# Retention, soft mixture of experts and a bilinear layer on one core: the first pair's k ahead of its tables, and the logits' exponential ahead of PV

## The chip, the cores and the metric

The kernel runs on one core of a Trainium2 chip. The core has five engines with an instruction row each: TensorE (PE; PEld is its weight load), VectorE (DVE), ScalarE (ACT), GpSimd (POOL) and SyncE (SP), which here issues the transfers; 16 DMA engines carry these. An engine takes its instructions strictly in the order in which they were written. The metric is the device time of one execution in microseconds (us).

## The reference

What is computed, cut to what matters (8 batches, 8 heads, 576 positions of 64 features, so 4608 tokens of 512):

```python
scores = np.matmul(q, k.transpose(0, 1, 3, 2)) / np.sqrt(64)
ret = scores * Dmat            # gamma_h ** (i - j) for i >= j, else 0
x = np.matmul(ret, v)          # then (4608, 512): tokens x (heads * 64)

logits = x @ phi               # 32 slots
d = np.exp(logits - logits.max(0)); d /= d.sum(0) + 1e-09
slot_input = d.T @ x           # 8 experts x 4 slots
for e in range(8):
    slot_out[e] = np.maximum(slot_input[e] @ w1[e], 0) @ w2[e]
c = np.exp(logits - logits.max(1, keepdims=True)); c /= c.sum(1, keepdims=True) + 1e-09
x = c @ slot_out

out = (((x @ m1) * (x @ m2)) @ w3) @ w_out
```

The weights m1, m2, w3 and w_out come as 64-bit floats and are converted on the chip (`conv_list`).

## The kernel before, in words

**Stages.** First the retention stage runs over 36 units of 128 tokens. Then the eight experts run over the 32 slots, with a product of w3 and w_out (`emit_Ws`) between them; then a small stage on the slots' pair products (`L955`, `L979`), and last nine output blocks of 512 tokens (`L1018` to `L1023`).

**Units.** A unit holds two chunks of 64 positions of one batch, all heads. Two units that hold the same chunks of two batches are a pair, and share one load each of q, k and v (512 KB each). Four pairs and one tail unit (the ninth chunk of both batches) make a group of 9 units; there are four groups. For a unit u TensorE does: `emit_kt` (four transposes of the scaled k, `L202`, copied to `kt` by ACT, `L203`), `emit_qk` (`L234`), masked by VectorE into `pm` (`emit_p`, `L244`), `emit_pv` (`L262`, into banks 5 and 3), `emit_state` (the running k-v product, `L275`, copied by ACT, `L282` or `L285`) and `emit_inter` (that state by q, `L295`, into banks 5 and 3 for the next unit). VectorE multiplies banks 5 and 3 by the factor table of the block into `xts` (`emit_xt`, `L308`); so `L295` must wait for `L308`. `emit_xtr` transposes `xts` and ACT copies it to `xg`.

**Scaling of k.** The raw rows of a pair, `kr` (two buffers), are multiplied by powers of gamma from the small table `ktab_sb` into `k` (`scale_k`: VectorE for the first pair, else GpSimd, `L189`, with ACT for two of the blocks, `L194`). A buffer of `kr` is free for load_k two pairs later when this is done. `xtab_sb` holds the factor tables of four blocks, made by GpSimd (`L659`) from the first and from `xstab`, a copy of the state table `stab_sb` with the two halves of the partitions swapped in every second column.

**Logits.** Every fourth unit, at the end of unit u with r = 1, `emit_logits` puts the logits of 512 tokens in one of three rotating banks (`misc_bank`), VectorE takes their running maximum and its negative `nm` (`L336` to `L343`). In the next unit (r = 2; u = 6, 10, ... 34) `emit_exp` on ACT makes the exponential `dd`, the correction `al` and the copy `lga` (`L357`), which is the last reader of the bank. The transposes of `emit_kt` of the unit after that need this bank.

**What sets the order.** `tc.manual_schedule()`: each engine's row is the order of the code. In every unit the loop emits, besides the above, pieces of the weight conversion (ACT `L469`, `L471`; VectorE `L470`, `L472`, `L464`; GpSimd `L490`, `L500`), and SP's requests for the pair three ahead and for the next weights. The expert weights go into the buffers that the retention stage leaves.

Of the kernel before, what the change touches and what calls it, by code (L numbers as in the profile page):

```python
# [15 lines left out]
ACTF = mybir.ActivationFunctionType  # L16
# [5 lines left out]
NU = NTOK // 128  # L22
# [9 lines left out]
def retention_softmoe_bilinear(  # L32
# [74 lines left out]
    ktab_sb = tabs_sb[:, 128:160].rearrange("p (c h k) -> p c h k", c=4, h=2)  # L107
# [238 lines left out]
    def emit_exp(T, keep=True):  # L346
        ps, nm, mn = st["lg"]
        lg = ps[:, 0:128]
        dd = tmp.tile([128, 128], F32, tag="dd", name="dd")
        zt = tmp.tile([128, 1], F32, tag="zt", name="zt", bufs=2)  # L350
        nc.scalar.activation(out=dd, in_=lg, func=ACTF.Exp, bias=nm, scale=1.0, accum_out=zt)
        al = None
        if T > 0:
            al = tmp.tile([128, 1], F32, tag="al", name="al", bufs=2)
            nc.scalar.activation(out=al, in_=st["m"], func=ACTF.Exp, bias=nm, scale=1.0)
        if keep:
            nc.scalar.copy(out=lga[:, T], in_=lg)  # L357
        st["m"] = mn
        st[T] = (dd, al, zt)
# [250 lines left out]
    with tc.manual_schedule():  # L610
        for i in range(2):
            for h in range(2):
                r = 64 * (1 - h)
                nc.sync.dma_start(out=ktab_sb[i:128:2, :, h], in_=tabs[r:r + 64, 256:292].rearrange("p (c k) -> p c k", k=4)[:, i:8:2])
        load_k(0)
        nc.sync.dma_start(out=cst[:, 0:160], in_=consts)
        load_q(0)
        nc.sync.dma_start(out=stab_sb, in_=tabs[:, 292:328].rearrange("p (c k) -> p c k", c=9))
        load_v(0)
        for r in range(2):  # L620
            for a, b in ((lo, hi), (hi, lo)) if r else ((slice(0, 128),) * 2,):
# [5 lines left out]
        for a, b in ((lo, hi), (hi, lo)):  # L627
            nc.sync.dma_start(out=ptail[a], in_=tabs[b, 0:256].rearrange("p (k i) -> p k i", k=4))
        for r in range(2):
            for a, b in ((lo, hi), (hi, lo)) if r else ((slice(0, 128),) * 2,):  # L630
                nc.sync.dma_start(out=phi_sb[a, r::2], in_=phi[b, r::2])
        nc.vector.memset(acc, 0.0)
        late = acc[:, 128:256]
# [29 lines left out]
        emit_kt(2)  # L663
# [13 lines left out]
        for u in range(NU):  # L677
            T, r = divmod(u - 4, 4)
            if first_of_pair(u + 4):
                scale_k(u + 4)  # L680
                load_k(pairs_in_order.index(units[u + 4][0]) + RBUF)
# [5 lines left out]
            if u + 3 < NU:  # L687
                emit_kt(u + 3)
            emit_pv(u)
            emit_xt(u)  # L690
            if u + 1 < NU:
                emit_state(u + 1)
            if u + 2 < NU:
# [23 lines left out]
            if u >= 6 and r == 2:  # L717
                emit_exp(T)
# [383 lines left out]
```

## Time and profile before

| | |
|---|---|
| timed runs | 429.08, 428.30, 425.40 us; median 428.3 |
| profiled execution | 425.7 us, its span 424.0 us |
| TensorE busy | 393.7 us (93%) |
| VectorE, ACT, GpSimd busy | 252.0, 198.2, 167.6 us |
| mean DMA rate | 255 GB/s |

The span runs from the first to the last instruction of the profiled execution. Busy time counts an engine's instructions; a matmul's end is modelled, since matmuls are pipelined. A releaser ("<-") is the work whose end let a waiting engine go on.

### The profile page before, as it was taken

The page shows a single profiled execution, that of the slowest core. Times are in us where ns is not written, and L with a number is a line of the kernel's source. Part 1 is how long each engine was busy: PE and PEld are TensorE (multiplying, and loading weights), DVE is VectorE, ACT ScalarE, POOL GpSimd, SP SyncE. Part 2 cuts the span into 40 slices and gives each one's busy share as a digit, 9 for nine tenths or more (in the row PEclk, how much of TensorE's full clock was granted, in tenths as well). Part 3 has the DMA queues.
Part 4 walks back from the last instruction along what each step waited for, and adds up shares of the span by engine and source line. Part 5 has one row for each costly group of instructions (what it writes and reads, how often), then busy time and mean ns, then how long its engine had stood idle before and what let it go on. Part 6 is the DMA issues. An engine that isn't in the chain of part 4 may idle for free.

```text
span 424.0 us, 11525 instructions
## 1 busy us (share of the span) xinstructions
PE 393.7 (93%) x4727; PEld 297.3 (70%) x4727; DVE 252.0 (59%) x492; ACT 198.2 (47%) x415; POOL 167.6 (40%) x149
## 2 busy tenths in 40 slices
PE   5589898999899898989999988899999999999996
PEld 2478786887777787866565544376888888888884
DVE  3335889788788886843777655048954443444310
ACT  2033677667656666532544432124454444545431
POOL 0151476564425444322344433102744434443410
PEclk9589999999999999999999999999999999999999
DMA  5889899779867967789899999967064898879633
GB/s 150 179 271 349 271 324 346 249 248 362 291 224 258 339 253 245 271 275 403 308 400 411 408 409 408 358 158 147 1 147 102 222 232 221 185 209 238 166 85 90
DMA packets 53076, 108.24 MB, mean 255 GB/s; under 512 B 12608, under 2 KB 15168, under 8 KB 53024
## 3 DMA queue, kind: packets, MB, share of 16 engines
q1 hardware_dynamic: 53024, 107.51, 79.1%
q8 instruction: 37, 0.61, 0.6%
q14 instruction: 15, 0.12, 0.1%
HBM read 96.87 MB, written 10.62 MB: 254 GB/s over the span
## 4 chain that ended last, share of the span: by engine, by line
PE 38%; DMA 10%; DVE 1%; ACT 1%; SPq 1%; issue 0%; ACTq 0%
PE bank L1018 8%; PE bank L1019 8%; PE bank L1020 8%; PE bank L955 5%; DMA k<-in_ew 5%; PE bank L531 3%; DMA kt<-in_ew 2%; DMA v<-in_ew 2%; PE bank L1021 2%; PE bank L577 2%; PE bank L558 1%; DMA lga<-expt 1%; PE bank L979 1%; DVE w L540 0%; SPq L592 0%
## 5 line engine op out<-in xcount | busy, mean ns | idle before, releaser
L602 POOL TENSOR_TENSOR cc<-mw_sb,cc 128x512 fp32r<-128x512 f32 x36 | 46.3, 1297 | 56.4 <-ACT cc L601 56.4
L490 POOL TENSOR_TENSOR vals<-vals,msb 128x512 int32<-128x512 int32 x24 | 30.8, 1283 | 59.5 <-DVE vals L464 34.5
L244 DVE TENSOR_TENSOR pm<-bank,msb 128x512 f32<-128x512 f32 x64 | 41.2, 684 | 16.9 <-PE bank L234 16.9
L600 DVE TENSOR_TENSOR mw_sb<-lga,raw 128x512 f32<-128x512 f32 x32 | 29.9, 956 | 34.9 <-POOL cc L602 28.4
L531 PE MATMUL bank<-wop,w3p 128*128 128x512 f32 x192 | 50.5, 406 | 0.0
L1023 ACT ACTIVATE mw_sb<-bank,rz 128x512 f32<-128x512 f32 x36 | 24.8, 689 | 51.4 <-PE bank L1021 28.9
L531 PEld LDWEIGHTS bank<-wop,w3p 128*128 128x128 f32 x192 | 34.2, 188 | 15.1 <-issue 8.7
L321 ACT COPY xg<-bank 128x512 f32<-128x512 f32 x34 | 19.9, 587 | 52.8 <-PE bank L320 52.7
L1018 PE MATMUL bank<-w3p,cc 128*128 128x512 f32 x108 | 42.4, 392 | 0.0
L1019 PE MATMUL bank<-w3p,cc 128*128 128x512 f32 x108 | 42.2, 391 | 0.0
L1020 PE MATMUL bank<-w3p,cc 128*128 128x512 f32 x108 | 42.2, 390 | 0.0
L234 PE MATMUL bank<-q,kt 64*64 64x128 f32 x1024 | 38.3, 285 | 1.1 <-DVE pm L244 0.8
L490 POOL TENSOR_TENSOR mw_sb<-mw_sb,msb 128x512 int32<-128x512 int32 x16 | 20.4, 1274 | 40.2 <-DVE mw_sb L464 31.2
L262 PE MATMUL bank<-pm,v 128*64 128x128 f32 x512 | 36.0, 283 | 0.1
L189 POOL TENSOR_TENSOR k<-kr,msb 128x512 f32<-128x512 f32 (+1 forms) x30 | 25.4, 866 | 23.5 <-DMA kr<-in_v 23.5
L202 PE MATMUL bank<-cst,k 128*128 128x128 f32 x128 | 21.1, 290 | 13.9 <-ACT lga L357 6.8
L500 POOL TENSOR_TENSOR w3p<-vals,w3p 128x512 fp32r<-128x512 f32 x16 | 20.5, 1283 | 33.6 <-ACT w3p L495 33.6
L234 PEld LDWEIGHTS bank<-q,kt 64*64 64x64 f32 x1024 | 29.7, 138 | 4.6 <-DVE pm L244 1.5
L262 PEld LDWEIGHTS bank<-pm,v 128*64 128x64 f32 x512 | 28.1, 139 | 5.9 <-issue 5.6
L471 ACT ACTIVATE msb<-raw 128x512 int32<-128x512 uint32 x40 | 27.8, 695 | 0.0
L202 PEld LDWEIGHTS bank<-cst,k 128*128 128x128 f32 x128 | 14.8, 146 | 17.9 <-ACT lga L357 6.3
L601 ACT CAST cc<-mw_sb 128x512 fp32r<-128x512 f32 x36 | 21.6, 618 | 11.4 <-DVE mw_sb L600 8.7
(190 smaller groups left out, 783.7 us busy)
## 6 DMA issues: line engine op xcount, KB each, us to landing
q<-in_q SPq DMA_DIRECT2D x20, 512.0 KB, 6.2
raw<-expt SPq DMA_DIRECT2D x36, 256.0 KB, 4.3
kr<-in_v SPq DMA_DIRECT2D x16, 512.0 KB, 5.5
v<-in_v SPq DMA_DIRECT2D x16, 512.0 KB, 6.8
raw<-in_m SPq DMA_DIRECT2D x16, 512.0 KB, 6.8
raw<-in_w SPq DMA_DIRECT2D x16, 512.0 KB, 6.2
out_x<-mw_sb SPq DMA_DIRECT2D x64, 128.0 KB, 2.8
k<-in_ew SPq DMA_DIRECT2D x14, 512.0 KB, 10.0
```

Source lines behind the costliest of these rows:

```text
L202: nc.tensor.transpose(ps[:, 128 * p:128 * p + 128], k_tile(u)[:, x, p].rearrange("p h j -> p (h j)"), ident)
L234: nc.tensor.matmul(out=ps[b, p], lhsT=ktb[u % 2][a, p, b], rhs=Q[a, :, x, p], start=True, stop=True)
L244: nc.vector.tensor_tensor(out=p_main(u)[:, h], in0=qk_view(h).rearrange("p (k t) -> p k t", k=4), in1=mask_sb.unsqueeze(1).to_broadcast([1 ...
L262: nc.tensor.matmul(out=xt_view(p)[side(p, h)], lhsT=v_tile(u)[:, 1 - h, x, p], rhs=p_main(u)[:, h, p], start=(block_of(u) == 0 and p < 2), ...
L471: lambda: nc.scalar.activation(out=p.bitcast(I32), in_=lo, func=ACTF.Copy, scale=2.0 ** -29),
L490: nc.gpsimd.tensor_tensor(out=ti, in0=ti, in1=parts[j % 2].bitcast(I32), op=ALU.add)
L531: nc.tensor.matmul(out=ps, lhsT=x, rhs=y, start=(k8 == 0 and part == 0), stop=(k8 == 7 and part == 2))
L600: eng.tensor_tensor(out=e, in0=x, in1=y[:, m], op=ALU.mult)
L602: nc.gpsimd.tensor_tensor(out=cl[m], in0=e, in1=ch[m], op=ALU.subtract)
L1018: nc.tensor.matmul(out=ob, lhsT=ch[m][:, sl], rhs=gh[m], start=(m == 0), stop=False)
L1019: nc.tensor.matmul(out=ob, lhsT=ch[m][:, sl], rhs=gl[m], start=False, stop=False)
L1020: nc.tensor.matmul(out=ob, lhsT=cl[m][:, sl], rhs=gh[m], start=False, stop=False)
```

## The change

It moves instructions and changes small transfers; the amount of arithmetic stays, but for one memset and two tables' multiplications that change engines.

At the start: SP's first request is the k of pair 0. The tables for k's scaling come in runs of 32 numbers (all blocks and both kinds of heads at once, of which every second is used) and, like the identity, by ACT's queue; the state table comes whole, in three transfers instead of four, and the swapped copy's even columns are copied by GpSimd. The second pair's k is requested fourth. The tail tables and phi are requested behind the third pair's loads. VectorE scales all four blocks of the first pair, in two halves, with the transposes of a half right behind it. The first unit's PV stands ahead of the second pair's transposes. A dummy exponential makes ACT load its table early.

In the loop: `emit_exp` stands ahead of `emit_pv` of its unit, and its copy `lga` ahead of `al`.

```diff
@@ the tables of k's scaling
-    ktab_sb = tabs_sb[:, 128:160].rearrange("p (c h k) -> p c h k", c=4, h=2)
+    ktab_rows = tabs_sb[:, 240:304].rearrange("p (h n) -> p h n", h=2)
+    ktab_sb = tabs_sb[:, 240:304].rearrange("p (h c i k) -> p c h i k", h=2, c=4, i=2)[:, :, :, 0]
@@ emit_exp
+        if keep:
+            nc.scalar.copy(out=lga[:, T], in_=lg)
         if T > 0:
             al = tmp.tile([128, 1], F32, tag="al", name="al", bufs=2)
             nc.scalar.activation(out=al, in_=st["m"], func=ACTF.Exp, bias=nm, scale=1.0)
-        if keep:
-            nc.scalar.copy(out=lga[:, T], in_=lg)
@@ ahead of the loop
+        load_k(0)
         for i in range(2):
             for h in range(2):
                 r = 64 * (1 - h)
-                nc.sync.dma_start(out=ktab_sb[i:128:2, :, h], in_=tabs[r:r + 64, 256:292].rearrange("p (c k) -> p c k", k=4)[:, i:8:2])
-        load_k(0)
-        nc.sync.dma_start(out=cst[:, 0:160], in_=consts)
+                nc.scalar.dma_start(out=ktab_rows[i:128:2, h], in_=tabs[r:r + 64, 256 + 4 * i:288 + 4 * i])
+        nc.scalar.dma_start(out=cst[:, 0:160], in_=consts)
         load_q(0)
-        nc.sync.dma_start(out=stab_sb, in_=tabs[:, 292:328].rearrange("p (c k) -> p c k", c=9))
         load_v(0)
+        load_k(1)
...
-                nc.sync.dma_start(out=xstab[a, :, r::2], in_=tabs[b, 292:328].rearrange("p (c k) -> p c k", c=9)[:, :, r::2])
-        load_k(1)
+                nc.sync.dma_start(out=(xstab if r else stab_sb)[a], in_=tabs[b, 292:328].rearrange("p (c k) -> p c k", c=9))
         load_q(1)
         load_v(1)
...
+        nc.scalar.activation(out=zacc, in_=acc[:, 0:1], func=ACTF.Exp)
...
-        scale_k(0, True)
+        first_k = rb[0].rearrange("p (h x k j) -> p h x k j", h=2, x=2, k=4)
+
+        def scale_first(x):
+            for h in range(2):
+                nc.vector.tensor_tensor(
+                    out=k_tile(0)[:, x, :, h], in0=first_k[:, 1 - h, x], in1=ktab_sb[:, 0, h].unsqueeze(2).to_broadcast([128, 4, 64]), op=ALU.mult,
+                )
+
+        scale_first(0)
+        emit_kt(0)
+        scale_first(1)
         load_k(2)
-        load_q(2)
-        load_v(2)
+        emit_kt(1)
...
-        nc.vector.memset(acc, 0.0)
-        emit_kt(0)
-        emit_kt(1, nc.vector.tensor_copy)
+        load_q(2)
+        load_v(2)
...
         emit_qk(0)
         emit_p(0)
-        nc.vector.tensor_tensor(
-            out=xtab_sb[0][:, :, 64:128], in0=xtab_sb[0][:, :, 0:64], in1=xstab[:, 1].unsqueeze(2).to_broadcast([128, 4, 64]), op=ALU.mult,
-        )
-        scale_k(2)
-        load_k(3)
-        for c in range(1, 4):
-            nc.gpsimd.tensor_tensor(out=xtab_sb[c], in0=xtab_sb[0], in1=xstab[:, 2 * c].unsqueeze(2).to_broadcast([128, 4, 128]), op=ALU.mult)
         emit_qk(1)
         emit_p(1)
         emit_state(0)
-        emit_kt(2)
+        nc.gpsimd.tensor_copy(xstab[:, :, 0::2], stab_sb[:, :, 0::2])
+        scale_k(2)
+        load_k(3)
+        for c in range(4):
+            o, n = (64, 64) if c == 0 else (0, 128)
+            nc.gpsimd.tensor_tensor(
+                out=xtab_sb[c][:, :, o:o + n], in0=xtab_sb[0][:, :, 0:n], in1=xstab[:, max(2 * c, 1)].unsqueeze(2).to_broadcast([128, 4, n]), op=ALU.mult,
+            )
@@ the loop over units (scale_k and load_k of unit u + 4 are next_k now, which unit 0 calls behind emit_kt(3))
-            if u + 3 < NU:
+            if 0 < u < NU - 3:
                 emit_kt(u + 3)
+            if u >= 6 and r == 2:
+                emit_exp(T)
             emit_pv(u)
+            if u == 0:
+                emit_kt(2)
             emit_xt(u)
             if u + 1 < NU:
                 emit_state(u + 1)
+            if u == 0:
+                emit_kt(3)
+                next_k()
...
-            if u >= 6 and r == 2:
-                emit_exp(T)
```

The places at which engines wait or are waited for, as rows of instructions (line numbers of the changed kernel are its own). SP's row at the very start of the program, before (kr_107 and kr_108 are the two buffers for raw k, q_101, q_102 and v_104, v_105 those of the first two pairs; msb holds the small tables, slotm the first factor table, cst the identity):

```order
L614 DMA msb<-in_tabs 64x4x4 x4
L162 DMA kr_107<-in_v 128x2x512
L616 DMA cst<-in_consts 128x160
L172 DMA q_101<-in_q 128x2x512
L618 DMA msb<-in_tabs 128x36
L178 DMA v_104<-in_v 128x2x512
L622 DMA slotm<-in_tabs 128x2x64
L623 DMA msb<-in_tabs 128x18x1
L622 DMA slotm<-in_tabs 64x2x64
L623 DMA msb<-in_tabs 64x18x1
L622 DMA slotm<-in_tabs 64x2x64
L623 DMA msb<-in_tabs 64x18x1
L162 DMA kr_108<-in_v 128x2x512
```

and in the changed kernel:

```order
L163 DMA kr_107<-in_v 128x2x512
L173 DMA q_101<-in_q 128x2x512
L179 DMA v_104<-in_v 128x2x512
L163 DMA kr_108<-in_v 128x2x512
L624 DMA slotm<-in_tabs 128x2x64
L625 DMA msb<-in_tabs 128x36
L624 DMA slotm<-in_tabs 64x2x64
L625 DMA msb<-in_tabs 64x36
L624 DMA slotm<-in_tabs 64x2x64
L625 DMA msb<-in_tabs 64x36
L173 DMA q_102<-in_q 128x2x512
L179 DMA v_105<-in_v 128x2x512
```

The second pair's k (kr_108) stood behind all tables and stands fourth now; the tables for k and the identity have left this row.

TensorE's row behind the `emit_qk` of units 0 and 1, before (bank_72 and bank_70 are the banks 5 and 3 of PV, bank_71 the state, bank_69 and bank_73 the rotating ones; v_104 is pair 0, k_110 the second pair's scaled k, pm_97 unit 0's masked product):

```order
L275 MATMUL bank_71<-v_104,k_109 64x64 x8
L202 MATMUL bank_69<-cst,k_110 128x128 x4
L202 MATMUL bank_73<-cst,k_110 128x128 x4
L262 MATMUL bank_72<-pm_97,v_104 64x128 x2
L262 MATMUL bank_70<-pm_97,v_104 64x128 x2
L262 MATMUL bank_72<-pm_97,v_104 64x128 x2
L262 MATMUL bank_70<-pm_97,v_104 64x128 x2
L275 MATMUL bank_71<-v_104,k_109 64x64 x8
```

and in the changed kernel:

```order
L276 MATMUL bank_71<-v_104,k_109 64x64 x8
L263 MATMUL bank_72<-pm_97,v_104 64x128 x2
L263 MATMUL bank_70<-pm_97,v_104 64x128 x2
L263 MATMUL bank_72<-pm_97,v_104 64x128 x2
L263 MATMUL bank_70<-pm_97,v_104 64x128 x2
L203 MATMUL bank_69<-cst,k_110 128x128 x4
L276 MATMUL bank_71<-v_104,k_109 64x64 x8
L203 MATMUL bank_73<-cst,k_110 128x128 x4
```

The second pair's eight transposes stood ahead of unit 0's PV, and stand behind it and behind `emit_state(1)` now.

ACT's row around the exponential of unit 10, before (kt from bank_74 is the copy of unit 13's transposes, xg_96 that of `emit_xtr`):

```order
L203 COPY kt<-bank_74 128x512
L321 COPY xg_96<-bank_69 128x512
L351 ACTIVATE dd,zt<-bank_73,nm 128x128
L355 ACTIVATE al<-mt,nm 128x1
L357 COPY lga<-bank_73 128x128
L471 ACTIVATE msb<-raw 128x512
L194 ACTIVATE k_110<-kr_108,msb 128x2x64 x2
L495 CAST wop<-vals 128x512
```

and in the changed kernel:

```order
L204 COPY kt<-bank_74 128x512
L352 ACTIVATE dd,zt<-bank_73,nm 128x128
L355 COPY lga<-bank_73 128x128
L358 ACTIVATE al<-mt,nm 128x1
L322 COPY xg_96<-bank_69 128x512
L472 ACTIVATE msb<-raw 128x512
L195 ACTIVATE k_110<-kr_108,msb 128x2x64 x2
L496 CAST wop<-vals 128x512
```

The exponential and the copy lga stood behind the xg copy, and stand right behind the kt copy now, lga ahead of al.

## Rows read from the trace of the kernel before

**Rows 1.** The page: busy us of each engine (share of the span) and instructions.

```profile
PE 393.7 (93%) x4727; PEld 297.3 (70%) x4727; DVE 252.0 (59%) x492; ACT 198.2 (47%) x415; POOL 167.6 (40%) x149
```

**Rows 2.** Timeline, 0 to 28 us: start, length, engine, line, work, [idle before <-releaser].

```profile
0.80 2.77 SPq L614 DMA_DIRECT2D msb<-in_tabs  x4
...
7.86 4.10 SPq L622 DMA_DIRECT2D slotm<-in_tabs  x1
...
8.95 0.44 PE L202 MATMUL bank<-cst,k 128*128 128x128 f32 x2 [2.01 <-DVE k L189]
...
10.24 0.58 ACT L203 COPY kt<-bank 128x512 f32<-128x512 f32 x1 [0.42 <-PE bank L202]
...
10.88 1.99 PE L234 MATMUL bank<-q,kt 64*64 64x128 f32 x32 [0.24 <-ACT kt L203]
...
14.07 0.72 SPq L162 DMA_DIRECT2D kr<-in_v  x1
...
16.14 1.12 PE L275 MATMUL bank<-v,k 128*64 128x64 f32 x16
...
19.43 1.61 POOL L189 TENSOR_TENSOR k<-kr,msb 128x512 f32<-128x512 f32 x2 [17.18 <-DMA kr<-in_v]
...
21.10 1.97 PE L202 MATMUL bank<-cst,k 128*128 128x128 f32 x8 [3.84 <-POOL k L189]
...
27.35 0.66 PE L202 MATMUL bank<-cst,k 128*128 128x128 f32 x4 [1.07 <-POOL k L189]
```

**Rows 3.** Windows: length, then busy us of each engine, PEclk, DMA share, GB/s.

```profile
10.00:11.00 1.00, 0.76 (x9) 0.52 (x13) 0.59 (x2) 0.58 (x1) 0.00 (x0) 0.91 1.10 323
12.00:16.00 4.00, 3.22 (x50) 2.33 (x44) 1.29 (x2) 0.00 (x0) 0.00 (x0) 0.50 0.50 22
17.30:21.10 3.80, 0.00 (x0) 0.00 (x1) 1.44 (x3) 0.69 (x2) 1.67 (x3) 0.50 1.02 364
21.10:24.24 3.14, 3.14 (x20) 2.81 (x22) 0.00 (x0) 0.59 (x1) 2.94 (x3) 0.50 0.83 251
23.00:186.00 163.00, 153.13 (x3301) 126.25 (x3304) 127.28 (x263) 99.33 (x226) 77.01 (x72) 1.00 0.83 285
```

**Rows 4.** TensorE's waits from 23 to 186 us: total, times, longest.

```profile
PE bank L202 <- ACT lga L357: 6.8, 5, 1.5
PE bank L295 <- DVE xts L308: 1.7, 2, 1.3
```

**Rows 5.** The chain that ended last: its first transfer of the expert stage.

```profile
227.51 10.14 DMA v<-in_ew
```

**Rows 6.** Windows again, in the expert stage.

```profile
205.00:210.00 5.00, 4.67 (x41) 2.19 (x44) 4.83 (x11) 2.87 (x7) 2.58 (x2) 1.00 0.67 241
```

**Rows 7.** Groups by form, 0 to 23 us: xcount, busy us, mean ns, idle before.

```profile
L659 POOL TENSOR_TENSOR slotm<-slotm,msb 128x512 f32<-128x512 f32 x1 | 1.0, 1042 | 0.0
...
L189 DVE TENSOR_TENSOR k<-kr,msb 128x256 f32<-128x256 f32 x1 | 0.4, 418 | 0.0
```

**Rows 8.** DMA issues up to 9 us: count, size, median us to landing.

```profile
kr<-in_v SPq DMA_DIRECT2D x1, 512.0 KB, 4.1
...
cst<-in_consts SPq DMA_DIRECT2D x1, 80.0 KB, 3.9
msb<-in_tabs SPq DMA_DIRECT2D x4, 4.0 KB, 2.2
...
msb<-in_tabs SPq DMA_DIRECT2D x1, 9.0 KB, 5.9
```

**Rows 9.** Timeline of units 10 and 11, and of unit 19 (last row).

```profile
67.48 0.15 DVE L343 TENSOR_SCALAR nm<-mn 128x1 f32<-128x1 f32 x1
...
71.72 0.26 ACT L357 COPY lga<-bank 128x128 f32<-128x128 f32 x1
...
72.18 1.66 DVE L464 SCALAR_TENSOR_TENSOR vals<-raw,vals 128x512 uint32<-128x512 uint32 x1
...
109.55 0.69 DVE L464 SCALAR_TENSOR_TENSOR mw_sb<-raw,mw_sb 128x512 uint32<-128x512 uint32 x1
```

More of the change, by code (lines that the diff above doesn't have):

```diff
@@ L610, in retention_softmoe_bilinear @@
     with tc.manual_schedule():
+        swap = lambda r: ((lo, hi), (hi, lo)) if r else ((slice(0, 128),) * 2,)
+        load_k(0)
         for i in range(2):
@@ L613, in retention_softmoe_bilinear @@
                 r = 64 * (1 - h)
-                nc.sync.dma_start(out=ktab_sb[i:128:2, :, h], in_=tabs[r:r + 64, 256:292].rearrange("p (c k) -> p c k", k=4)[:, i:8:2])
-        load_k(0)
-        nc.sync.dma_start(out=cst[:, 0:160], in_=consts)
+                nc.scalar.dma_start(out=ktab_rows[i:128:2, h], in_=tabs[r:r + 64, 256 + 4 * i:288 + 4 * i])
+        nc.scalar.dma_start(out=cst[:, 0:160], in_=consts)
         load_q(0)
-        nc.sync.dma_start(out=stab_sb, in_=tabs[:, 292:328].rearrange("p (c k) -> p c k", c=9))
         load_v(0)
+        load_k(1)
         for r in range(2):
-            for a, b in ((lo, hi), (hi, lo)) if r else ((slice(0, 128),) * 2,):
+            for a, b in swap(r):
                 nc.sync.dma_start(out=xtab_sb[0][a, r::2, 0:64], in_=tabs[b, 328:584].rearrange("p (k i) -> p k i", k=4)[:, r::2])
-                nc.sync.dma_start(out=xstab[a, :, r::2], in_=tabs[b, 292:328].rearrange("p (c k) -> p c k", c=9)[:, :, r::2])
-        load_k(1)
+                nc.sync.dma_start(out=(xstab if r else stab_sb)[a], in_=tabs[b, 292:328].rearrange("p (c k) -> p c k", c=9))
         load_q(1)
         load_v(1)
[L627 to L631, printed above, removed]
         nc.vector.memset(acc, 0.0)
+        nc.scalar.activation(out=zacc, in_=acc[:, 0:1], func=ACTF.Exp)
         late = acc[:, 128:256]
@@ L647, in retention_softmoe_bilinear @@
         nc.vector.scalar_tensor_tensor(out=mask_sb, in0=mask_sb, scalar=even, in1=late, op0=ALU.mult, op1=ALU.add)
-        nc.vector.memset(acc, 0.0)
-        emit_kt(0)
-        emit_kt(1, nc.vector.tensor_copy)
+        load_q(2)
+        load_v(2)
+        for a, b in swap(1):
+            nc.sync.dma_start(out=ptail[a], in_=tabs[b, 0:256].rearrange("p (k i) -> p k i", k=4))
+        for r in range(2):
+            for a, b in swap(r):
+                nc.sync.dma_start(out=phi_sb[a, r::2], in_=phi[b, r::2])
         emit_qk(0)
         emit_p(0)
-        nc.vector.tensor_tensor(
-            out=xtab_sb[0][:, :, 64:128], in0=xtab_sb[0][:, :, 0:64], in1=xstab[:, 1].unsqueeze(2).to_broadcast([128, 4, 64]), op=ALU.mult,
-        )
-        scale_k(2)
-        load_k(3)
-        for c in range(1, 4):
-            nc.gpsimd.tensor_tensor(out=xtab_sb[c], in0=xtab_sb[0], in1=xstab[:, 2 * c].unsqueeze(2).to_broadcast([128, 4, 128]), op=ALU.mult)
         emit_qk(1)
@@ L678, in retention_softmoe_bilinear, with next_k @@
             T, r = divmod(u - 4, 4)
-            if first_of_pair(u + 4):
-                scale_k(u + 4)
-                load_k(pairs_in_order.index(units[u + 4][0]) + RBUF)
+            def next_k():
+                if first_of_pair(u + 4):
+                    scale_k(u + 4)
+                    load_k(pairs_in_order.index(units[u + 4][0]) + RBUF)
+            if u > 0:
+                next_k()
             run(subs)
@@ L692, in retention_softmoe_bilinear @@
                 emit_state(u + 1)
+            if u == 0:
+                emit_kt(3)
+                next_k()
             if u + 2 < NU:
```

## The prediction

> **What bounds the kernel now.** I read the page's busy times first [rows 1]: TensorE is busy for 393.7 of 424.0 us, so a change gains only where TensorE stands still or runs at its lower clock. Next, the timeline of the first 28 us [rows 2]: TensorE ends its first piece of work (the transposes of units 0 and 1, both `emit_qk`, `emit_state(0)`) at 16.14 + 1.12 = 17.26 and then stands still for 3.84 us, until GpSimd has scaled the second pair's k, for which GpSimd in turn waited for the transfer. That k was requested only at 14.07: SyncE had four row tables to issue ahead of the first k (2.77 us), and later one table whose issue took 4.10 us. Unit 1 waits another 1.07 us for the third pair's k. The windows [rows 3] show what the queue was doing: from 12 to 16 us the DMA engines are busy for half the time and move 22 GB/s, against 364 GB/s from 17.3 to 21.1. That is where the state tables for `xstab` come in, in runs of 4 bytes. The same windows show the granted clock: 0.91 between 10 and 11 us, and still 0.50 (the lower level, 1.2 GHz) from 21.1 to 24.24, at the end of which it rises, TensorE having worked without a gap since 21.10.
>
> Behind that, the waits of TensorE from 23 to 186 us [rows 4] are nearly all that is left to gain in the retention stage: 6.8 us in five waits of a transpose `L202` for ACT's copy `L357`, and 1.7 us for `L308`. With the 1.07 us above this agrees with the row over that stage [rows 3]: TensorE busy for 153.1 of 163 us.
>
> Last, the chain of waits: from 227.5 us it goes through transfers of expert weights, some 10 us each [rows 5], so the expert stage is bound by DMA. Does it absorb what the first stage gains? Its transfers start when TensorE frees a buffer; from 205 to 210 us the DMA engines are busy for 0.67 of the time [rows 6], so until then it is not DMA that sets the pace. The saturated part begins when the work ahead lets it, and moves earlier as a whole. I take a shift of the first stage as a shift of the end, one for one.
>
> **The change part by part.** *The wait for the second pair's k: 3.84 us.* load_k(1) is now SP's fourth issue; at the 0.7 us that each of the four tables took to issue (2.77), it is issued by about 2.8. Behind k, q and v, 2.1 MB in all at 364 GB/s from about 2.9, it lands at 9 to 10. Also, PV(0) no longer stands behind its transposes in TensorE's row, and needs only P(0) and the first pair's v. The 3.84 us go entirely.
>
> *The start of the chain: 1.2 us.* The first transposes began at 8.95, and qk(0) at 10.88, right behind the copy of kt(0) (0.58). Now the scaling is four VectorE multiplications of 256 elements at 0.42 [rows 7], of which the first two release kt(0); ACT's two are gone. k(0) is issued at 0.8 and lands 4.1 us later [rows 8], at 4.9; ktab goes out on ACT's queue, four issues in 2.8 us, landing 2.2 us behind the last [rows 8], at about 5.6. Scaling of x = 0 is done by 6.6. Then the identity, which the transposes need, comes last: fifth in ACT's queue, issued at about 3.6. With its old 3.9 us [rows 8] it lands at 7.5. But it now shares the engines with 2.1 MB instead of with k(0) alone; were it served only after all of that, it would land at 10.0. I take 8.2, near the first, because at its old place it also had 512 KB ahead of it. Four transposes at 0.22 (two took 0.44) end at 9.1, and qk(0) begins at 9.7, 1.2 us earlier. Bounds: 1.9 earlier to 0.7 later. The copy of kt(1) moves from VectorE to ACT, behind that of kt(0): 0.58 us, wanted only by qk(1), so nothing.
>
> The Trainium skill, page "DMA: Bandwidth & Descriptors", section "Issuing engines are not separate DMA queues", says that transfers started by different engines end up on the same 16 DMA engines and interleave, so that a second issuing engine saves only the time of issuing. No trace here shows a second queue. By that rule what ACT's queue brings is SP's 2.77 us, and the identity's transfer is drawn out by what it interleaves with; the first rival works that out from rows.
>
> *The clock: 1.5 us.* If it falls at 10.9 again, qk(0), begun at 9.7, has 1.2 us at the full clock ahead of that and needs the lower level for less: 0.5 us saved. The 3.14 us to 24.24 [rows 3] ran at the lower level behind a gap; that work now follows state(0) with no gap ahead of it, so the clock should rise sooner. Half of it, 1.57, could be saved; I take 1.0. Bounds: nothing, and, if the clock never falls, half of the 6.4 us from 10.88 to 17.26 and 1.57, 4.8 in all.
>
> *Unit 1's wait for the third pair's k: 1.07 us.* k(2) is requested at 9 to 10, not behind all tables. But GpSimd's row is longer ahead of it: a copy of 18 columns (no row shows one; between nothing and the 1.04 of a 512-column table [rows 7], I take 0.3, since it is small), scale_k(2) 1.61, half a table 0.5, three tables at 1.04, scale_k(4) 1.61. The copy waits for the last of six table transfers, issued at 6.5 and landing up to 5.9 us later [rows 8]: 12.4. That makes 14.3 for scale_k(2), 17.9 for the tables, 19.6 for scale_k(4). The place of 21.10 is now 15.5 (less 3.84, 1.2 and half a us of clock); what lay from there to 27.35 less the wait, 5.2 us, makes unit 1's transposes due at 20.7. So the wait goes, with a cover of 1.1 us; the table for xt(0) is ready at 14.8, wanted at 17. If the cover is gone, up to 1 us comes back.
>
> Start in sum: 3.84 + 1.2 + 1.5 + 1.07 = 7.6 us; with the bounds 3.84 - 0.7 = 3.1 and 3.84 + 1.9 + 4.8 + 1.07 = 11.6.
>
> *Tail tables and phi behind the third pair's loads:* five issues, some 3.1 us of SP, now ahead of load_k(3) instead of load_k(2). k(3), issued at about 14, is due in unit 3, near 28: nothing. *VectorE's second memset of `acc` and its table product* stood beside TensorE's work: nothing; were they in the way, half a us each. *The early exponential* moves ACT's table load ahead of the first work, into the wait for data: nothing.
>
> *The exponential ahead of PV: 5.1 us.* In unit 10 the negated maximum `nm` is ready at 67.63, but `lga` is copied from 71.72 [rows 9], since both exponentials stand behind the xg copy, and TensorE waits for that. Moved, exponential and copy come some 3 us earlier, and the transpose finds its bank free. The five waits average 1.36 us. In three of the units VectorE's conversion is over in time (in unit 19 at 109.55 + 0.69 = 110.24), so they go whole: 4.1. In units 7 and 11 VectorE is late as well: `L464` takes 1.66 us and ends at 73.84, so the xt product cannot begin much earlier than now, and TensorE's next `L295` waits for it. I take 0.5 each: 4.1 + 1.0 = 5.1. Bounds 3.0 and 6.8. ACT's state copies come a little later for it; they are used a unit later, with a cover of over 2 us: nothing.
>
> **Sum.** 7.6 + 5.1 = 12.7 us off the profiled execution's 425.7 gives 413.0. The timed runs of before lie at 425.4 to 429.1, their median, 428.3, 2.6 above that execution. I put half of that on top: 414.3, so **414 us**.
>
> **The rivals.** (1) *The identity comes late*, as the rule on interleaving would have it: it lands at 10.0, qk(0) comes 0.7 us later than before, while the wait for k goes. 1.9 us less gain, 416. For it: 2.1 MB in flight around it; against: it needs 80 KB. 0.12. (2) *VectorE takes over the exponential's gain*: behind each removed wait TensorE stands at `L295` for `L308`, as it does twice already [rows 4]. 5.1 us less, 419. For it: VectorE is busy for 127 of 163 us; against: in three units of five it was in time. 0.14. (3) *DMA takes the start back*: units that come earlier find their raw pieces late, ACT's `L469` blocks its row, or the expert stage stays where it was. 7.6 less, 422. Against: 0.83 of DMA over the stage, 0.67 ahead of the saturated part. 0.09. (4) *Slower, by ACT's order*: the exponential waits for `nm` from VectorE, and the state copies, k's scaling and the next kt copy stand behind it. If TensorE waits w for that in each of nine units, the time is 425.7 - 7.6 - 6.8 + 9w + 1.3; it decides from w = 1.6 us, and w = 2.4 gives 434. For it: `L464` can take 1 us longer; against: `nm` was ready 3.5 us before its exponential ran. 0.05. (5) *Nothing comes of it*, both waits being replaced by others: 426 to 430, 0.04.
>
> **How the numbers follow.** The forecast has 0.56. With its bounds (gains of 6 to 18, the offset 0 to 2.6) it lies between 408 and 422; most of it and rivals 1 and 2 lie in **408.5 to 421**, which leaves out some 0.2. A measurement of this kernel tells about 1% from no change. Faster by over 1% (below 424): the forecast and rivals 1 to 3, 0.91; within 1%: 0.04; slower: 0.05.
>
> **What would show it.** The start: no idle time ahead of the second pair's transposes, PV(0) near 15.5 instead of 23, the clock at 1.00 before 20 us. The exponential: the waits for `lga` gone from TensorE's list, those for `L308` not above 3.5 us. The shift: the expert stage begins about 12 us earlier, and the chain through its transfers is as long as before. I am wrong if the identity or `nm` appears as a releaser, if `L308` takes over the five waits, or if the expert transfers begin earlier but end where they did.

## The result, and the profile after

| | before | changed |
|---|---|---|
| timed runs, median of 4 | 427.28 us (425.4 to 429.08) | 414.67 us (414.31 to 417.3) |
| ratio | 1 | 0.9719 [0.9656, 0.9781] |
| profiled execution, its span | 425.71, 424.0 us | 415.01, 413.3 us |

The kernel became 2.8% faster, 12.6 us by the medians (the 428.3 us that stand ahead are the median of three of the four runs of before); the two profiled executions are 10.7 us apart in span. The page's busy line for the changed kernel answers to [rows 1]:

```profile
PE 392.5 (95%) x4727; PEld 297.5 (72%) x4727; DVE 253.1 (61%) x491; ACT 198.3 (48%) x415; POOL 168.4 (41%) x151
```

TensorE's work is nearly the same (392.5 us, 393.7 before), the span shorter: the gain lies in its idle time and in its clock. The timeline of the first 28 us of the changed kernel (columns as in [rows 2]):

```profile
0.80 2.51 ACTq L617 DMA_DIRECT2D msb<-in_tabs  x4
...
0.81 0.77 SPq L163 DMA_DIRECT2D kr<-in_v  x1
...
3.02 0.61 SPq L163 DMA_DIRECT2D kr<-in_v  x1
3.35 0.61 ACTq L618 DMA_DIRECT2D cst<-in_consts  x1
...
7.14 0.43 DVE L642 TENSOR_TENSOR k<-kr,msb 128x256 f32<-128x256 f32 x1 [4.46 <-DMA msb<-in_tabs]
...
8.69 1.10 DVE L642 TENSOR_TENSOR k<-kr,msb 128x256 f32<-128x256 f32 x3 [1.12 <-DMA msb<-in_tabs]
...
9.61 1.94 PE L203 MATMUL bank<-cst,k 128*128 128x128 f32 x8 [2.67 <-DMA cst<-in_consts]
...
11.47 1.99 PE L235 MATMUL bank<-q,kt 64*64 64x128 f32 x32
...
17.64 1.79 PE L263 MATMUL bank<-pm,v 128*64 128x128 f32 x16
18.64 1.61 POOL L190 TENSOR_TENSOR k<-kr,msb 128x512 f32<-128x512 f32 x2 [1.27 <-DMA kr<-in_v]
...
19.37 0.66 PE L203 MATMUL bank<-cst,k 128*128 128x128 f32 x4
...
21.15 1.10 PE L235 MATMUL bank<-q,kt 64*64 64x128 f32 x32
...
22.19 0.69 PE L203 MATMUL bank<-cst,k 128*128 128x128 f32 x4
```

Nothing stands still ahead of the second pair's transposes any more (19.37, right behind PV(0); before: 3.84 us of waiting), nor ahead of unit 1's (22.19; before 27.35 with 1.07 of waiting). GpSimd now waits 1.27 us for the third pair's k and is done at 18.64 + 1.61 = 20.25, 1.9 us ahead of TensorE. But `emit_qk` of unit 0 starts at 11.47, later than the 10.88 of before: the chain ahead of it waits for the small tables (VectorE at 7.14, and again at 8.69) and for the identity (TensorE at 9.61).

Two windows of the changed kernel (columns as in [rows 3]): one us in that start, and the stretch from PV(0) to 1.75 us behind the start of the last unit's PV, the same work as the last row of [rows 3] but for 24 matmuls more, the second pair's eight transposes among them:

```profile
11.00:12.00 1.00, 1.00 (x15) 0.67 (x17) 0.00 (x0) 0.73 (x2) 0.07 (x1) 1.00 0.29 55
17.64:176.15 158.51, 154.39 (x3325) 127.86 (x3326) 129.44 (x264) 100.16 (x227) 75.98 (x70) 1.00 0.86 293
```

In the second row TensorE works 154.4 of 158.5 us; it was 153.1 of 163. The idle time fell from 9.9 to 4.1 us, and 1.07 of that fall is the wait of unit 1. Of the two entries in TensorE's list of waits in [rows 4] one is left, from 13 to 175 us (total, times, longest):

```profile
PE bank L296 <- DVE xts L309: 3.2, 5, 1.3
```

The five waits for `lga` (6.8 us) are gone; those of `L296` for the xt product rose from 1.7 us in two to 3.2 in five. In unit 10 the copy `lga` starts 0.6 us behind the maximum's end, where it stood 4.1 us behind it [rows 9]; timeline of the changed kernel:

```profile
62.60 0.15 DVE L344 TENSOR_SCALAR nm<-mn 128x1 f32<-128x1 f32 x1
...
63.34 0.25 ACT L355 COPY lga<-bank 128x128 f32<-128x128 f32 x1
```

The first expert transfer in the chain that ended last (start, length), against [rows 5]:

```profile
217.41 10.15 DMA v<-in_ew
```

It starts 10.1 us earlier and takes as long as before.

### The profile page after: what moved, and what is told of

Same layout as the page of the kernel before. It is cut to its first block, busy times and chain, and to the rows that moved or that the text cites. A ratio compares the mean times of both kernels' runs of the same rounds, so it can differ in the third digit from the quotient of the medians.

```text
span 413.3 us, 11533 instructions
## 1 busy us (share of the span) xinstructions
PE 392.5 (95%) x4727; PEld 297.5 (72%) x4727; DVE 253.1 (61%) x491; ACT 198.3 (48%) x415; POOL 168.4 (41%) x151
## 4 chain that ended last, share of the span: by engine, by line
PE 40%; DMA 10%; DVE 2%; ACT 1%; issue 0%; ACTq 0%; SPq 0%; DVEq 0%
PE bank L1037 8%; PE bank L1038 8%; PE bank L1039 8%; PE bank L974 5%; DMA k<-in_ew 5%; PE bank L532 4%; DMA kt<-in_ew 2%; DMA v<-in_ew 2%; PE bank L1040 2%; PE bank L578 2%; PE bank L559 1%; PE bank L998 1%; PE bank L915 1%; DVE w L541 0%; ACT w L540 0%
## 5 line engine op out<-in xcount | busy, mean ns | idle before, releaser
L204 ACT COPY kt<-bank 128x512 f32<-128x512 f32 x32 | 18.6, 581 | 17.8 <-PE bank L203 17.8
L296 PE MATMUL bank<-q,st 64*64 64x128 f32 (+1 forms) x512 | 21.7, 263 | 3.2 <-DVE xts L309 3.2
```

## The experiments

All times are medians; each group of runs had the kernel before on the same chip, at 426.96, 426.28 and 426.36 us. The table shows where the profiled execution of each kernel stood: the starts of PV in units 0, 1 and 35 by the timelines, and the span (us).

| kernel | PV of unit 0 | unit 1 | unit 35 | span | span less unit 35 | timed | ratio to before |
|---|---|---|---|---|---|---|---|
| before | 23.00 | 27.94 | 184.25 | 424.0 | 239.8 | 427.28 | 1 |
| changed | 17.64 | 22.80 | 174.40 | 413.3 | 238.9 | 414.67 | 0.9719 [0.9656, 0.9781] |
| start only | 17.41 | 22.55 | 181.24 | 420.9 | 239.7 | 419.98 | 0.9843 [0.9802, 0.9883] |
| exponential only | 24.71 | 28.95 | 181.67 | 420.6 | 238.9 | 422.9 | 0.9903 [0.987, 0.9935] |
| transposes ahead | 17.05 | 20.39 | 172.63 | 411.7 | 239.1 | 413.66 | 0.9692 [0.9664, 0.972] |
| tables by SP | 17.38 | 22.98 | 178.27 | 417.8 | 239.5 | 419.21 | 0.979 [0.9725, 0.9854] |
| k request only | 17.56 | 28.10 | 187.42 | 426.8 | 239.4 | 427.62 | 1.0028 [1.0002, 1.0054] |
| short runs | 17.91 | 22.83 | 176.15 | 414.8 | 238.7 | 417.7 | 0.9808 [0.9762, 0.9853] |
| no dummy | 16.00 | 20.63 | 171.47 | 410.4 | 238.9 | 414.29 | 0.9728 [0.9701, 0.9756] |
| small first | 14.73 | 22.29 | 176.51 | 415.3 | 238.8 | 417.09 | 0.9807 [0.976, 0.9853] |
| factors late | 13.22 | 22.44 | 176.54 | 415.6 | 239.1 | 417.3 | 0.976 [0.9718, 0.9802] |
| changed, again | 16.03 | 20.88 | 177.26 | 416.3 | 239.0 | 416.54 | 0.9753 [0.971, 0.9796] |

The sixth column is read first: from the last unit's PV to the end every kernel takes 238.7 to 239.8 us, however early that PV comes. So what the retention stage gains arrives at the end, to within 1.1 us.

**Start only** (e1_start_only): the changed kernel with the exponential back at its old place.

```diff
-        if keep:
-            nc.scalar.copy(out=lga[:, T], in_=lg)
         if T > 0:
...
             nc.scalar.activation(out=al, in_=st["m"], func=ACTF.Exp, bias=nm, scale=1.0)
+        if keep:
+            nc.scalar.copy(out=lga[:, T], in_=lg)
...
-            if u >= 6 and r == 2:
-                emit_exp(T)
             emit_pv(u)
...
                 emit_dT(T)
+            if u >= 6 and r == 2:
+                emit_exp(T)
             run_conv(1)
```

> The changed kernel with the exponential back at its old place (behind the xg copy, lga behind al): the start alone. Theory A (two independent savings that simply add): unit 1's transposes at 22.2 as in the changed kernel, the five waits of the transposes for lga back with 6 to 7 us in total, time about 5 us above the changed kernel, near 420. Rival B (the exponential's saving is only visible because the start moved, or is absorbed by the xt product): time within 1.5 us of the changed kernel, near 415.

It measured 419.98 us. TensorE's waits from 13 to 186 us in this kernel are those of before:

```profile
PE bank L203 <- ACT lga L358: 6.8, 5, 1.5
PE bank L296 <- DVE xts L309: 1.7, 2, 1.3
```

The changed kernel's ratio is 0.0124 lower, 5.3 us of 427: that is the exponential's worth on top of the start.

**Exponential only** (e2_exp_only): the kernel before with that move alone.

```diff
         al = None
+        if keep:
+            nc.scalar.copy(out=lga[:, T], in_=lg)
         if T > 0:
...
-        if keep:
-            nc.scalar.copy(out=lga[:, T], in_=lg)
         st["m"] = mn
...
                 emit_kt(u + 3)
+            if u >= 6 and r == 2:
+                emit_exp(T)
             emit_pv(u)
...
-            if u >= 6 and r == 2:
-                emit_exp(T)
             run_conv(1)
```

> The kernel before with the exponential moved ahead of PV (lga ahead of al) and nothing else. Theory A: the five waits for lga go, those for the xt product grow from 1.7 to about 3.2 us, 4.5 to 5 us less than before, near 422. Rival B: VectorE takes over what is removed, waits for the xt product grow by 5 us or more, time as before, near 427.

It measured 422.9 us. TensorE's waits over the same stretch:

```profile
PE bank L202 <- POOL k L189: 6.7, 1, 6.7
PE bank L295 <- DVE xts L308: 2.8, 5, 1.3
```

The waits for `lga` are gone, the xt products hold TensorE up for 2.8 us in five waits, and the start shows its wait for the second pair's k (6.7 us here, 3.84 in the trace of before: in this execution the work ahead of it ended 1.2 us sooner, at 16.1, and GpSimd got that k 1.7 us later, at 21.14). The two parts alone give 1.57% and 0.97%, together 2.54%; the change gives 2.81%, so within the intervals they add up. That VectorE would take the exponential's gain over, the second rival, is wrong but for the 1.1 to 1.5 us by which the xt waits grew.

**Transposes ahead** (e3_kt_ahead): the second pair's transposes back ahead of unit 0's PV.

```diff
-            emit_pv(u)
             if u == 0:
                 emit_kt(2)
+                emit_kt(3)
+            emit_pv(u)
...
-                emit_kt(3)
                 next_k()
```

> The changed kernel with the second pair's eight transposes ahead of unit 0's PV again, all else kept. Theory A (the early request for k is what removed the 3.84 us): that k is scaled at 13.7, long before state(0) ends at 17.9, so TensorE does not wait, the order is worth nothing, time within 0.7 us of the changed kernel. Rival C (the order of PV and transposes removed the wait): TensorE waits again ahead of the transposes and the time is 2 to 4 us longer, 417 to 419.

It measured 413.66 us, and its timeline has no wait at that place:

```profile
16.03 1.09 PE L203 MATMUL bank<-cst,k 128*128 128x128 f32 x8
...
17.05 1.09 PE L263 MATMUL bank<-pm,v 128*64 128x128 f32 x16
```

Once k comes in time, the order of PV and transposes is worth nothing that these runs can show: the move of PV is no part of the gain. (This execution was ahead in the start because its matmuls reached their short length sooner, which the last section comes to.)

**Tables by SP** (e4_tables_by_sp): the tables for k and the identity in SP's queue again, around the first k.

```diff
-        load_k(0)
         for i in range(2):
             for h in range(2):
-                nc.scalar.dma_start(out=ktab_rows[i:128:2, h], in_=tabs[r:r + 64, 256 + 4 * i:288 + 4 * i])
-        nc.scalar.dma_start(out=cst[:, 0:160], in_=consts)
+                nc.sync.dma_start(out=ktab_rows[i:128:2, h], in_=tabs[r:r + 64, 256 + 4 * i:288 + 4 * i])
+        load_k(0)
+        nc.sync.dma_start(out=cst[:, 0:160], in_=consts)
         load_q(0)
```

> The changed kernel with the tables for k (still in long runs) and the identity back in SP's queue: the four tables ahead of the first k, the identity behind it; k of the second pair still fourth of the large loads. Theory A (interleaving with 2 MB of rows made the tables and the identity late): first k lands about 7.5, the identity before 9, first transposes at 8.7 to 9.2 instead of 9.61, qk(0) at 10.5 to 11.0 instead of 11.47, time the same or up to 1 us shorter. Rival D (SP's issue time is what counts): everything begins 2.5 us later, qk(0) near 14, time 2 to 3 us longer, 417 to 418.

It measured 419.21 us. The first rows of TensorE's chain:

```profile
8.25 1.97 PE L203 MATMUL bank<-cst,k 128*128 128x128 f32 x8 [1.32 <-DVE k L642]
...
11.22 1.98 PE L235 MATMUL bank<-q,kt 64*64 64x128 f32 x32 [0.99 <-DMA q<-in_q]
```

The transposes start 1.36 us earlier than with ACT's queue, as tables and identity land sooner; but q, requested later, now holds up `emit_qk` for 0.99 us, and unit 1's PV comes at 22.98, as in the changed kernel (22.80). In the start of this execution the queue that the small tables use is worth nothing. But GpSimd gets the state tables later and scales the third pair's k later, and TensorE waits 0.31 us for that:

```profile
20.72 1.61 POOL L190 TENSOR_TENSOR k<-kr,msb 128x512 f32<-128x512 f32 x2
...
140.87 0.33 PE L321 MATMUL bank<-cst,xts 128*128 128x128 f32 x1 [2.19 <-issue]
```

That k is done at 20.72 + 1.61 = 22.33 and at 20.25 in the changed kernel, which the section on the prediction comes back to. The time is 4.5 us above that of the changed kernel; neither forecast had that. In the profiled execution 4.0 of that lie in units 26 and 27, where TensorE stands still for 2.19 us at 138.7 with no releaser (the last row) and then works at half its speed; no edit touches that place. Whether the other executions lost theirs in the same way the runs do not show.

**k request only** (e5_k_early_only): the kernel before, with the second pair's k requested fourth of the raw rows and nothing else changed.

```diff
         load_v(0)
+        load_k(1)
         for r in range(2):
...
-        load_k(1)
         load_q(1)
```

> The kernel before with one edit: the second pair's k is requested ahead of the factor and state tables instead of behind them. Theory E (SP's whole row is what is late, so the next k takes over): the 3.84 us go, but the third pair's k is still requested at about 20 us and scaled at about 27, so unit 1's PV stays near 27.5 (27.94 before, 22.80 changed) and the time falls by less than 1 us, near 426. Rival F (the one request was the whole wait): unit 1's PV near 24, time 3.5 to 4 us shorter, near 423.

It measured 427.62 us: nothing is gained. The timeline:

```profile
20.88 1.50 PE L234 MATMUL bank<-q,kt 64*64 64x128 f32 x32 [1.76 <-DMA q<-in_q]
...
25.39 1.61 POOL L189 TENSOR_TENSOR k<-kr,msb 128x512 f32<-128x512 f32 x2 [2.24 <-DMA kr<-in_v]
...
27.06 1.11 PE L202 MATMUL bank<-cst,k 128*128 128x128 f32 x4 [4.68 <-POOL k L189]
```

PV(0) comes at 17.56 (23.00 before), so the wait of 3.84 us is gone; but the third pair's k is requested no sooner, behind the same tables, and so 1.76 us of waiting for q and 4.68 for that k take its place, and unit 1's PV starts at 28.10. That the wait for the second k is all that stands in the way is refuted here; the whole of SP's row had to move.

**Short runs** (e6_short_runs): the changed kernel with the state tables in 4-byte runs again, four transfers, and no copy on GpSimd.

```diff
         load_k(1)
+        nc.sync.dma_start(out=stab_sb, in_=tabs[:, 292:328].rearrange("p (c k) -> p c k", c=9))
...
-                nc.sync.dma_start(out=(xstab if r else stab_sb)[a], in_=tabs[b, 292:328].rearrange("p (c k) -> p c k", c=9))
+                nc.sync.dma_start(out=xstab[a, :, r::2], in_=tabs[b, 292:328].rearrange("p (c k) -> p c k", c=9)[:, :, r::2])
...
-        nc.gpsimd.tensor_copy(xstab[:, :, 0::2], stab_sb[:, :, 0::2])
```

> The changed kernel with the state tables in runs of 4 bytes again (one whole table and three part tables by SP, no copy on GpSimd). Theory E: SP's row stands still for some 4 us at these, so q, v of the second pair and k of the third come 4 to 6 us later than in the changed kernel; unit 1's transposes wait for the third k and its PV comes at 24 to 27 instead of 22.80; time 1.5 to 4 us longer, 416 to 419. Rival G (with the second k ahead of them the tables do no harm): unit 1's PV at 22.8, time as the changed kernel, 414.5.

It measured 417.7 us. The timeline:

```profile
8.24 2.19 SPq L625 DMA_DIRECT2D slotm<-in_tabs  x1
...
14.07 0.61 SPq L163 DMA_DIRECT2D kr<-in_v  x1
...
20.32 1.61 POOL L190 TENSOR_TENSOR k<-kr,msb 128x512 f32<-128x512 f32 x2 [1.04 <-DMA kr<-in_v]
...
22.22 0.69 PE L203 MATMUL bank<-cst,k 128*128 128x128 f32 x4
```

SP is held up for 2.19 us at one issue (4.10 before, [rows 2]) and asks for its next k at 14.07; yet unit 1 is not late (PV at 22.83, changed 22.80). So in this execution the longer runs are worth nothing in the start; but that is narrow. The third pair's k is scaled at 20.32 + 1.61 = 21.93, 1.7 us later than in the changed kernel (20.25) and 0.3 ahead of TensorE; had TensorE reached its higher speed as early as in e10, where these transposes start at 20.29, it would have waited. The median lies 3.0 us above the changed kernel's. The changed program ran at 413.6 to 419.1 in its ten executions, but on the chip of this run e7, the changed kernel but for the early exponential, took 412.1 to 415.1 us and this one 416.5 to 419.9. These don't overlap, so the loss doesn't look like chance, and this trace shows only a part of it.

**No dummy** (e7_no_dummy): the early exponential left out.

```diff
-        nc.scalar.activation(out=zacc, in_=acc[:, 0:1], func=ACTF.Exp)
```

> The changed kernel without the dummy exponential. Theory of the prediction (it lies in the wait for data, worth nothing): time as the changed kernel. Rival H (the table load then runs when ACT's first copy has its data, and the copy of kt(0) behind it): copy of kt(0) 1.28 us later, qk(0) at 12.7 instead of 11.47, time 1.3 us longer; the timeline decides, since the times alone tell 1 us only just.

It measured 414.29 us, the same as with it, and the timeline shows why:

```profile
3.98 1.28 ACT L204 ACT_TABLE_LOAD   x1 [3.98 <-issue]
...
13.96 1.60 PE L235 MATMUL bank<-q,kt 64*64 64x128 f32 x32 [0.88 <-DVE pm L245]
```

ACT loads its table at 3.98, long before its first copy, without the dummy as well.

**Small first** (e8_small_first): the factor and state tables requested ahead of the first v and the second k.

```diff
         load_q(0)
-        load_v(0)
-        load_k(1)
         for r in range(2):
...
+        load_v(0)
+        load_k(1)
         load_q(1)
```

> The changed kernel with SP's six table transfers ahead of v of the first and k of the second pair, so that only k and q of the first pair (1 MB instead of 2) are in flight beside the tables and the identity. Theory A (interleaving made these late): identity at 8.0 instead of 9.57, qk(0) at about 9.9 instead of 11.47, PV(0) at about 16, unit 1's PV at 21.2; time 1.5 us shorter, near 413. Rival I (their lateness comes from ACT's queue itself): qk(0) stays at 11 to 11.5 and the later k costs up to 1 us: 414.5 to 416.

It measured 417.09 us. The timeline:

```profile
7.93 1.97 PE L203 MATMUL bank<-cst,k 128*128 128x128 f32 x8 [1.00 <-DVE k L642]
...
9.83 1.99 PE L235 MATMUL bank<-q,kt 64*64 64x128 f32 x32
...
21.69 0.66 PE L203 MATMUL bank<-cst,k 128*128 128x128 f32 x4 [2.48 <-POOL k L190]
...
22.29 1.98 PE L263 MATMUL bank<-pm,v 128*64 128x128 f32 x16
```

With 1 MB of raw rows in flight beside the identity instead of 2, `emit_qk` starts at 9.83, 1.64 us earlier, and PV(0) at 14.73, 2.9 earlier. The 1.64 us are the price of the second MB (the first table comes no sooner: VectorE begins at 7.12, in the changed kernel at 7.14). But they are not kept: TensorE waits 0.54 us for the second pair's k again, the third pair's k is ready at 21.7, 1.4 us later than in the changed kernel, TensorE waits 2.48 us for it, and unit 1's PV runs for 1.98 us behind that gap (1.09 for PV(0) in e3, at full speed). Unit 1 gains half a us, and the time is not the 413 of theory A but 2.4 us above the changed kernel's.

**Factors late** (e9_k_ahead_of_factors): the same, and three of GpSimd's factor tables behind the scaling of the third pair's k.

```diff
+        factor(0)
...
                 next_k()
+                for c in range(1, 4):
+                    factor(c)
```

> The kernel with the small tables first (six table transfers ahead of v of the first and k of the second pair) and, besides, GpSimd's three factor tables behind the scaling of the third pair's k. Theory J (with the small tables first, what was late next was GpSimd's row: 3.1 us of factor tables ahead of the third k's scaling, which cost 2.5 us of waiting and then the clock): the wait of unit 1's transposes falls from 2.5 us to under 0.7, unit 1's PV at 20.0 to 20.6 instead of 22.3, time 2 to 2.5 us below the changed kernel, 412 to 413. Rival K (the third k's transfer itself comes at 20): the wait stays at 2 us or more and the time at 415 to 417.

It measured 417.3 us. The timeline:

```profile
20.19 1.61 POOL L190 TENSOR_TENSOR k<-kr,msb 128x512 f32<-128x512 f32 x2 [3.26 <-DMA kr<-in_v]
...
21.85 0.66 PE L203 MATMUL bank<-cst,k 128*128 128x128 f32 x4 [2.55 <-POOL k L190]
```

GpSimd is free, and waits 3.26 us for the transfer; TensorE is idle for 2.55, as in e8 (and for 2.14 ahead of the second pair's transposes). So it was not GpSimd's row that held the k back but the transfer itself, with the DMA engines busy for 0.93 of the time from 12 to 24 us. From there on the start is bounded by the raw rows' coming in. None of the variants is shown to beat the changed kernel.

**Changed, again** (e10_changed_again): the changed kernel as it is, beside the last one.

> The changed kernel once more, word for word, for a second trace of the same program. If TensorE's pauses without a releaser (1 to 2 us each in several runs) and the moment at which its matmuls reach full speed belong to the single execution, they stand elsewhere in this trace, PV(0) to unit 1's PV takes 4.6 to 5.6 us, and the times spread over 3 us again around 414.7. If they belong to the program, this trace has the same units at the same lengths as the first.

It measured 416.54 us. Its timeline in the start (both `emit_qk` and unit 1's transposes), to be read beside that of the first execution:

```profile
11.29 1.82 PE L235 MATMUL bank<-q,kt 64*64 64x128 f32 x32
...
13.99 1.60 PE L235 MATMUL bank<-q,kt 64*64 64x128 f32 x32 [0.88 <-DVE pm L245]
...
20.29 0.66 PE L203 MATMUL bank<-cst,k 128*128 128x128 f32 x4 [0.39 <-POOL k L190]
```

`emit_qk` of unit 0 starts 0.18 us earlier than in the first execution and unit 1's transposes 1.90 earlier, with 0.39 us of waiting among them: between the two, TensorE was at its higher speed sooner (1.60 for the second `emit_qk`, not 2.48). PV(0) to unit 1's PV takes 4.85 us, as expected; the six times spread over 5.5 us, not 3, around 416.5. From unit 1's PV to unit 35's this execution needs 156.4 us and the first 151.6; the last section shows where.

## Why the prediction was right, and where it was not

The mechanism was right: both gains came, they add up, and they reach the end one for one. Profile to profile I had 12.7 us, and it was 10.7; the offset to the median that I added (1.3) was -0.3. The two errors nearly cancel, so that 414 was met to 0.7 us is in part luck. By the terms:

| term | predicted | measured |
|---|---|---|
| wait for the second pair's k | 3.84 | 3.84 |
| unit 1's wait for the third k | 1.07 | 1.07; 0.68 in the second execution |
| start of the chain | 1.2 (-0.7 to 1.9) | -0.6; -0.4 in the second |
| clock | 1.5 (0 to 4.8) | 0.8; 2.9 in the second |
| start in sum | 7.6 | 5.2; 7.1 in the second |
| exponential | 5.1 (3.0 to 6.8) | 4.7; not to be seen in the second |

The measured start is the way from `emit_qk(0)` to unit 1's transposes, 16.47 us before, 10.72 and 9.00 in the two executions of the changed kernel: less the two waits, the rest, 0.84 and 2.95, is put down to the clock, with any other small gap in it. The exponential's term is what unit 35 gained beyond unit 1: 9.85 - 5.14; the last 0.85 of the 10.7 lies behind it.

**The wait for k** went as worked out, but I had not seen how much hung on the rest of SP's row: the k alone brings nothing. I had counted 3.84 and 1.07 as two separate terms; the second would have been 4.68 without the other moves.

**The step that failed** is the identity's and the tables' landing. I let the identity keep its 3.9 us [rows 8], "near the first, because at its old place it also had 512 KB ahead of it". The DMA issues of the changed kernel up to 9 us (count, size, median us from issue to landing):

```profile
cst<-in_consts ACTq DMA_DIRECT2D x1, 80.0 KB, 6.1
msb<-in_tabs ACTq DMA_DIRECT2D x4, 8.0 KB, 4.4
```

Issued at 3.35, the identity took 6.1 us, and TensorE began at 9.61 (I took 8.2 for the landing), released by the identity, which I had named as a sign of being wrong; the small tables took 4.4 us, not 2.2 (2.0 in e4, where they are issued ahead of all bulk), so that the second of the two multiplications for x = 0, which I had done by 6.6, began at 8.69. In the second execution it is this multiplication that releases TensorE, at 9.43: both came late. Of the 1.8 us by which `emit_qk(0)` missed my 9.7, 1.4 lie here; the other 0.4 are that it stands behind all eight transposes (1.86 us from the first one's start), not behind four and a copy (1.5). This is the mechanism of the first rival, which I gave 0.12: the small transfers shared the DMA engines with 2 MB of raw rows. It agrees with the rule of the Trainium skill that the prediction weighs (page "DMA: Bandwidth & Descriptors", section "Issuing engines are not separate DMA queues"). With 1 MB beside them instead, in e8, the chain starts 1.64 us earlier. The rival priced its loss at 1.9 us against the forecast, and the chain's start came out 1.8 off (1.2 against -0.6). Where I went wrong is that size alone says little: 512 KB ahead in the same queue had cost the identity less than 2 MB beside it.

**The exponential** came out 0.4 us from the forecast in this pair of executions, but its split was wrong. By the starts of PV in the timelines, the ways from unit 18 to 19, from 26 to 27 and from 30 to 31 became 1.65, 1.60 and 1.59 us shorter, 4.84 in all, where I had 4.1. I expected units 7 and 11 to gain 0.5 each. From unit 6 to 7 the way is 1.41 shorter, but from 7 to 8 it is 1.10 longer, which leaves 0.31; from 10 to 12 it is 10.08 us, 10.14 before. There VectorE takes over nearly all, the mechanism of the second rival: the xt waits grew by 0.55 in unit 7, 0.60 in unit 11 and 0.31 in unit 10. The two errors cancel. In the second execution the way from unit 1 to unit 35 is as long as before (156.4 and 156.3 us), since pauses fill it. What doesn't hang on one trace is e2's ratio: 4.1 us (2.8 to 5.6); e1 against the changed kernel gives 5.3, within wider bounds.

**What I costed at nothing** was nothing where a run tells it apart: the dummy exponential (e7) and the place of PV (e3). Of the longer runs (e6) and of ACT's queue (e4) the same holds in the start of the executions traced. The place of the tail tables and phi, the longer runs of k's tables and the scaling in two halves no run takes alone.

**Left open**: why the medians of e4 and e6 lie 3 to 4.5 us above the changed kernel's although their traced starts are equal to its first one. A part fits the third pair's k. Where it is scaled by 20.3 us (changed, e3, e7, e10), the times are 413.7 to 416.5; where it is scaled at 21.6 to 22.3 (e4, e6, e8, e9), 417.1 to 419.2. The first execution of the changed kernel reached its higher speed late, so that this k had 1.9 us of cover. In e10 unit 1's transposes start at 20.29, right behind it; my estimate for an execution like that one is a loss of 1.6 us with e6's k (21.93) and of 2.0 with e4's (22.33). That the untraced executions lost their time so is not shown.

## What to carry to other kernels

Taking away one wait in a row of requests moves it to the next request in that row: reorder the row as a whole, and ask for each of the next two or three items when it will land. Small transfers that a second engine issues still share the DMA engines with the bulk, so what the first instruction needs should have little in flight beside it. And when a rotating buffer holds up the engine that bounds the kernel, move the buffer's last reader ahead of work that doesn't need it; where the stage behind starts from the buffers that this one frees, the gain reaches the end whole.

## What the runs showed of the hardware that I had not expected

**Pauses without a releaser.** In e10 TensorE stops in the middle of 32 equal matmuls; the timeline of unit 8:

```profile
51.41 0.44 PE L235 MATMUL bank<-q,kt 64*64 64x128 f32 x5
...
53.54 1.78 PE L235 MATMUL bank<-q,kt 64*64 64x128 f32 x27 [1.69 <-issue]
...
55.25 1.93 PE L415 MATMUL bank<-xg,dt 128*32 128x512 f32 x8
```

Five matmuls, 1.69 us of nothing, for which the trace names no work that it waited for, and then 27 matmuls that take 1.78 us, at half speed. Two windows of the same stretch:

```profile
52.00:53.00 1.00, 0.00 (x0) 0.00 (x0) 0.40 (x2) 0.62 (x2) 1.00 (x1) 1.00 0.97 324
...
54.00:55.00 1.00, 1.00 (x23) 0.92 (x15) 0.04 (x1) 0.00 (x0) 1.00 (x3) 0.50 1.00 375
```

The granted clock is 1.00 during the pause and 0.50, the lower level (1.2 GHz), behind it; the unit took 7.98 us instead of 4.35. The DMA engines are full in both windows (0.97, 1.00). The first execution of the changed kernel has one pause up to 190 us, e10 has three, of which this is the second:

```profile
36.66 0.54 PE L235 MATMUL bank<-q,kt 64*64 64x128 f32 x9 [0.85 <-issue]
...
141.45 0.33 PE L321 MATMUL bank<-cst,xts 128*128 128x128 f32 x1 [1.39 <-issue]
```

With the slow unit behind the longest one they make up most of the 4.8 us between these two executions from unit 1 to unit 35. The places are not chance. The last row's stands at the same instruction as e4's pause of 2.19 us, and e3, e6 and e8 stop there too; e1, e4 and e6 stop ahead of the nine matmuls of the first row. From 20 to 190 us ten of the twelve traces have 27 such pauses. Counted through TensorE's instructions (matmuls, weight loads and its semaphore instructions) each stands at a multiple of 256 plus 193 to 196: the first row's at 962, e4's and e10's last at 5314. So the program sets where TensorE can stop, and the execution at which of these places it does and for how long (0.17 to 2.19 us). In 24 of the 27 pauses the DMA engines were busy for 0.92 of the time or more. What TensorE waits for there no run shows.

**When the higher speed comes differs between executions** of the same instructions: the second `emit_qk` took 2.48 us in the first execution of the changed kernel and 1.60 in the second, in e7 and in e3; PV(0) comes at 17.64 in the first, and at 16.03 and 16.00 in the second and in e7. The difference is as large as a term of the sum (0.8 against 2.9 us).

**The record of the granted clock has gaps.** In the first execution of the changed kernel it reads 1.00 from 11 to 12 us, while 32 matmuls of `emit_qk` took 1.99 us there, as long as those of before, and 1.10 for the same work at 21.15. The length of equal matmuls is the surer sign.
